# Tokens dealt four to a partition in a state-space layer gated by a GEGLU feed-forward

## The chip, the cores and the metric

The kernel runs on one core of a Trainium2 chip. The metric is the device time of one execution in microseconds (us); smaller is better. A second kind of time is used throughout: the span, from the first to the last instruction of one execution that the hardware profiler recorded.

## What is computed

x has 2048 tokens of 512 channels, in bf16. Cut to what matters, the reference is:

```python
xn = layernorm(x)                                   # per token, over 512 channels
Lam_bar = exp(dt * Lam);  B_bar = ((Lam_bar - 1) / Lam)[:, None] * B      # complex, 512 states
Bu = xn @ B_bar.T
for t in range(2048):                               # the recurrence runs over the tokens in order
    h = Lam_bar * h + Bu[t];  hs.append(h)
s = 2 * real(hs @ C.T) + xn * Dskip
g = silu((gelu(xn @ w_gate) * (xn @ w_up)) @ w_down)      # 512 -> 1376 -> 512
out = x + s * g
```

## The kernel before

The 2048 tokens are worked in four slabs of 512 (index `s`), each slab in four tiles of 128 tokens (index `m`). A tile puts its 128 tokens on the 128 partitions: before, tile `m` of slab `s` holds tokens 512s+128m to 512s+128m+127, so one partition holds one token of each tile.

- Loads. `load_x` (call at L222) brings the first slab as four transfers of one tile, `load_slab` (L217) the three others as one transfer each. Both read rows of one token, 1 KB, into `x_tok`.
- Normalized tokens go through a DMA transpose (`dma_t4`, L360) into `xnT`, channels on the partitions and tokens along the free axis, tile by tile. The first slab's feed-forward uses transposes on TensorE instead (L313, L328).
- Feed-forward, one tile after another: `gate_tile` makes the up and gate products (matmuls at L434; the first slab's are at L383 and L402), ScalarE copies them out of PSUM (L437), VectorE multiplies them (L443, L445), a DMA transpose turns the product (`at_t`, L450), and `down_pair` makes the down product (L466) and its Silu (L469).
- State part: `half(s, h)` makes, for half of the states, the products of B with all 512 tokens of the slab (matmuls at L532, one PSUM bank of 512 columns each, channels of the state on the partitions and tokens along the columns). ScalarE copies each bank into the tile `U` as bf16 (L534, eight copies in a slab, 32 in all). VectorE rotates `U` (L544, L556; L552 in the first slab) so that the recurrence becomes real, runs the scan along the tokens (L563), and rotates back into `hst`. The scan needs the tokens of `U` in their order in time.
- `y_tile` and `y_part` make y for a tile: eight matmuls (L482) whose stationary operand is the tile's 128 columns of `hst` and whose moving operand is C; a copy of the skip term stands in the bank beforehand (L478). VectorE multiplies with g (L487), adds x (L493), and a store follows (L498). The very last tile is made in two halves of 256 columns.

PSUM has eight banks: six form a ring that the products of L434, L466 and L532 take in turn, two (`ybank`) belong to y. A product can start only when the copy of the ring's former product from its bank is done. The statistics of the later slabs run on ScalarE (L744), as do their normalizations (L749).

The order of the work is written out as a list, `ORDER`, which is the same in both kernels: it fixes the sequence of instructions on every engine and in every DMA queue. TensorE is PE below, its weight loads (of stationary operands) PEld, VectorE DVE, ScalarE ACT.

Of the kernel before, what the change touches and what calls it, by code (L numbers as in the profile page):

```python
# [10 lines left out]
AF = mybir.ActivationFunctionType  # L11
# [6 lines left out]
PE, ACT, DVE, POOL, SP = "PE", "ACT", "DVE", "POOL", "SP"  # L18
# [62 lines left out]
def kernel(  # L81
# [17 lines left out]
    nc = tc.nc  # L99
    P = 128  # L100
# [5 lines left out]
    NPT = 4  # L106
    H2 = NPT // 2
    TS = 512
    NS = S // TS
    M = TS // P  # L110
# [10 lines left out]
    V, A, G, T = nc.vector, nc.scalar, nc.gpsimd, nc.tensor  # L121
    act = A.activation
# [5 lines left out]
    def sb(name, shape, dt=BF16):  # L128
        return consts.tile(shape, dt, name=name)

    x_tok = sb("x_tok", [P, NS * M, D])
# [5 lines left out]
    C2 = sb("C2", [P, 2, NPT, D])  # L137
    pv0, pv1 = sb("pv0", [4, P]), sb("pv1", [8, P])
    Drow = sb("Drow", [P, D])
    hst = [sb(f"hst{i}", [P, 2, NPT, TS]) for i in range(2)]  # L140
# [7 lines left out]
    U = [sb(f"U{i}", [P, 2, H2, TS]) for i in range(NU)]  # L148
# [11 lines left out]
    ot = [sb(f"ot{i}", [P, D]) for i in range(2)]  # L160
# [21 lines left out]
    def acts(n, emit, reads=(), writes=(), ptr=0, **kw):  # L182
        return pl.add(ACT, AC + 0.12 * ptr + n / 1200.0, emit, reads, writes, lag=0.16, **kw)
# [7 lines left out]
    def dma(eng, issue, land, emit, reads=(), writes=(), **kw):  # L191
        return pl.add(eng, issue, emit, reads, writes, lag=land, **kw)

    TURN, SLAB = (3, 2.28, 1.5), (2, 1.5, 1.0)
    x_r = A_x[0].rearrange("(m p) d -> p m d", p=P)
    out_td = out[0]
    w_of = {
        "wg": (wg, B_w_gate.rearrange("(k p) f -> p k f", p=P)),
        "wu": (wu, B_w_up.rearrange("(k p) f -> p k f", p=P)),
# [4 lines left out]
    def dma_sp(end, landed, emit, writes, **kw):  # L204

        n = dma(SP, end - sp_at[0], landed - end, emit, writes=writes, after=list(sp_last), not_before=sp_at[0], svc=(1, 0.0, 0.0), **kw)
        sp_at[0] = end
        sp_last[:] = [n]
# [5 lines left out]
               [(nm, k, c) for k in range(k0, k1) for c in range(3) if c0 <= CH[c][0] < c1])  # L214

    def load_slab(s, **kw):
        dma(SP, 0.8, 4.0, lambda: nc.sync.dma_start(out=x_tok[:, s * M : (s + 1) * M, :], in_=x_r[:, s * M : (s + 1) * M, :]),  # L217
            writes=[("x", s, m) for m in range(M)], svc=SLAB, **kw)


    def load_x(m, end, landed):
        dma_sp(end, landed, lambda: nc.sync.dma_start(out=x_tok[:, m, :], in_=x_r[:, m, :]), [("x", 0, m)])  # L222

    W2 = CH[1][1]
    load_x(0, 1.12, 2.92)
# [247 lines left out]
    def y_part(s, m, c0, c1, bank, key, seed, e):  # L473

        w = c1 - c0
        ps = bank[:, 0:w]
        if seed:
            acts(w, lambda: act(out=ps, in_=sk[s % 2][:, m, c0:c1], func=AF.Copy), [("sk", s % 2, m)], [key])  # L478

        def f():  # L480
            for j in range(2 * NPT):
                T.matmul(ps, lhsT=hst[s % 2][:, j // NPT, j % NPT, m * P : (m + 1) * P], rhs=C2[:, j // NPT, j % NPT, c0:c1],  # L482
                         start=(j == 0 and not seed), stop=(j == 2 * NPT - 1), skip_group_check=True)
        pe(2 * NPT, w, f, [("hst", s % 2, 0), ("hst", s % 2, 1)] + C2S + ([key] if seed else []), [key])
        gi, b = g2s[s, m]
        if seed:
            dve(w, lambda: V.tensor_tensor(out=yg[e][:, c0:c1], in0=ps, in1=g2[gi][:, b, c0:c1], op=ALU.mult), [key, ("g2", gi, b)], [("yg", e, c0)])  # L487
        else:
            ys = tF[:, 0, c0:c1]
            dve(w, lambda: V.tensor_tensor(out=ys, in0=ps, in1=sk[s % 2][:, m, c0:c1], op=ALU.add), [key, ("sk", s % 2, m)], [("tF",)])  # L490
            dve(w, lambda: V.tensor_tensor(out=yg[e][:, c0:c1], in0=ys, in1=g2[gi][:, b, c0:c1], op=ALU.mult), [("tF",), ("g2", gi, b)], [("yg", e, c0)])
        o = 2 + m % 2 if s == NS - 1 and m >= M - 2 else m % 2
        dve(w, lambda: V.tensor_tensor(out=ot[o][:, c0:c1], in0=yg[e][:, c0:c1], in1=x_tok[:, s * M + m, c0:c1], op=ALU.add),  # L493
            [("yg", e, c0), ("x", s, m)], [("ot", o, c0)], rate=2.0)
        mg = s * TS + m * P
        cuts = (0, HD) if (NS - 2, M - 2) <= (s, m) < (NS - 1, M - 2) else (c0,)
        for lo, hi in zip(cuts, (*cuts[1:], c1)):
            dma(SP, 0.35, 1.5, lambda lo=lo, hi=hi: nc.sync.dma_start(out=out_td[mg : mg + P, lo:hi], in_=ot[o][:, lo:hi]), [("ot", o, c0)], [("out", s, m, lo)], svc=(2, 0.4, 0.9))  # L498

    def y_tile(s, m):  # L500
        i = y_n[0] % 2
# [20 lines left out]
    def half(s, h):  # L522
        ui = u_n[0] % NU
        u_n[0] += 1
        for q in range(H2):
            pt = h * H2 + q
            for ri in range(2):
                r, ps = bank()

                def f(ri=ri, pt=pt, ps=ps):  # L530
                    for k in range(KT):
                        T.matmul(ps[:], lhsT=BT[:, ri, k, pt * P : (pt + 1) * P], rhs=xnT[:, s % 2, :, k, :], start=(k == 0), stop=(k == KT - 1))  # L532
                pe(KT, 512, f, [("BT", ri)] + [("xnT", s % 2, m) for m in range(M)], [("bank", r)])
                acts(512, lambda q=q, ri=ri, ps=ps: act(out=U[ui][:, ri, q, :], in_=ps[:], func=AF.Copy), [("bank", r)], [("U", ui, q, ri)])  # L534
        WQ = [P, 2, 2, H2 * TS]
        hs = slice(h * H2, (h + 1) * H2)
        Uf = U[ui][:].rearrange("p r q t -> p r (q t)")
        Wf = W[:].rearrange("p r q t -> p r (q t)")
        Ff = Fs[:].rearrange("p r q t -> p r (q t)")
        Qf = Q[:].rearrange("p j r q t -> p j r (q t)")  # L540
        tf = tab[:, :, hs, :].rearrange("p (j r) q t -> p j r (q t)", j=2)

        def rot(src, table, reads):
            dve(4096, lambda: V.tensor_tensor(out=Qf, in0=src.unsqueeze(1).to_broadcast(WQ), in1=table, op=ALU.mult),  # L544
                reads, ["Q"], rate=2.0)

        def turn(src, dst, reads, writes, back):
            if s == 0:
                rot(src, tf[:, :, 0, :].unsqueeze(2).to_broadcast(WQ), reads + ["tab0", "tab2"])
                for ri in range(2):  # L550
                    op = ALU.add if (ri == 0) == back else ALU.subtract
                    dve(1024, lambda ri=ri, op=op: V.tensor_tensor(out=dst[:, ri, :], in0=Qf[:, 0, ri, :], in1=Qf[:, 1, 1 - ri, :], op=op),  # L552
                        ["Q"], writes, rate=2.0)
            else:
                rot(src, tf[:, :, ::-1, :] if back else tf, reads + TABS)
                dve(2048, lambda: V.tensor_tensor(out=dst, in0=Qf[:, 0, :, :], in1=Qf[:, 1, ::-1, :], op=ALU.add), ["Q"], writes, rate=2.0)  # L556

        turn(Uf, Wf, [("U", ui, q, ri) for q in range(H2) for ri in range(2)], ["W"], True)
        for q in range(H2):
            for ri in range(2):  # L560
                pt = h * H2 + q
                first = 0.0 if s == 0 else ini[h][:, ri, q : q + 1]
                pl.add(DVE, 1.12 if s == 0 else 1.185, lambda ri=ri, q=q, pt=pt, first=first: V.tensor_tensor_scan(  # L563
                    out=Fs[:, ri, q, :], data0=rho[:, pt : pt + 1].to_broadcast([P, TS]), data1=W[:, ri, q, :], initial=first,
                    op0=ALU.mult, op1=ALU.add), ["W", "rho", ("ini", h)], [("F", ri, q)], lag=0.13)
        allf = [("F", ri, q) for ri in range(2) for q in range(H2)]
        if s < NS - 1:
            fl = Fs[:, :, :, TS - 1]
            Wc = [P, 2, H2]
            it = ini[h]  # L570

            def carry():
                V.tensor_tensor(out=ta[:], in0=fl, in1=cS[:, hs].unsqueeze(1).to_broadcast(Wc), op=ALU.mult)
                V.tensor_tensor(out=tb[:], in0=fl, in1=sS[:, hs].unsqueeze(1).to_broadcast(Wc), op=ALU.mult)
                V.tensor_tensor(out=it[:, 0, :], in0=ta[:, 0, :], in1=tb[:, 1, :], op=ALU.subtract)
                V.tensor_tensor(out=it[:, 1, :], in0=ta[:, 1, :], in1=tb[:, 0, :], op=ALU.add)
            pl.add(DVE, 0.42, carry, allf + ["trig"], [("ini", h)], lag=0.13)
        turn(Ff, hst[s % 2][:, :, hs, :].rearrange("p r q t -> p r (q t)"), allf, [("hst", s % 2, h)] + (CTS if s == 1 else []), False)
# [102 lines left out]
    c1, s1 = cbt[:, :, 1], sbt[:, :, 1]  # L681
# [32 lines left out]
    for pt in range(NPT):  # L714
# [3 lines left out]
            out=C2[:, 0, pt, :], in0=CT[:, 0, pt, :], scalar=cre[:, pt : pt + 1], in1=tF[:, 1, :], op0=ALU.mult, op1=ALU.subtract),  # L718
            ["coef", ("CT", 0), ("tF",)], [("C2", 0, pt)], base=0.13)
        dve(512, lambda pt=pt: V.scalar_tensor_tensor(  # L720
            out=C2[:, 1, pt, :], in0=CT[:, 1, pt, :], scalar=ncre[:, pt : pt + 1], in1=tF[:, 0, :], op0=ALU.mult, op1=ALU.subtract),
# [104 lines left out]
```

## Time and profile before

| what | value |
|---|---|
| median of 3 runs | 179.13 us (178.66 to 179.43) |
| the profiled execution: time, span | 178.61 us, 176.8 us |
| PE busy | 171.7 us, 97% of the span |
| weight loads busy (beside PE) | 82.7 us, 47% |
| DVE busy | 156.4 us, 88% |
| ACT busy | 125.1 us, 71% |
| granted clock of TensorE | 1.0 |
| DMA packets | 48083, 18.66 MB |

The 1.8 us between span and time lie ahead of the first and behind the last instruction. Busy shares are means over stages that differ: the first 25 us belong to the first slab's feed-forward, and the four state parts start near 24, 38, 72 and 107 us. Groups of instructions are named by line, engine and operation; a matmul's own duration includes its way through the array, while the next one starts earlier.

### The profile page before, as it was taken

The page shows a single profiled execution, that of the slowest core. Times are in us where ns is not written, and L with a number is a line of the kernel's source. Part 1 is how long each engine was busy: PE and PEld are TensorE (multiplying, and loading weights), DVE is VectorE, ACT ScalarE, POOL GpSimd, SP SyncE. Part 2 cuts the span into 40 slices and gives each one's busy share as a digit, 9 for nine tenths or more (in the row PEclk, how much of TensorE's full clock was granted, in tenths as well). Part 3 has the DMA queues.
Part 4 walks back from the last instruction along what each step waited for, and adds up shares of the span by engine and source line. Part 5 has one row for each costly group of instructions (what it writes and reads, how often), then busy time and mean ns, then how long its engine had stood idle before and what let it go on. Part 6 is the DMA issues. An engine that isn't in the chain of part 4 may idle for free.

```text
span 176.8 us, 2414 instructions
## 1 busy us (share of the span) xinstructions
PE 171.7 (97%) x834; PEld 82.7 (47%) x850; DVE 156.4 (88%) x252; ACT 125.1 (71%) x240; POOL 12.0 (7%) x25
## 2 busy tenths in 40 slices
PE   7999999999999999999999999999999999999992
PEld 2555544444455544444445454444444455444451
DVE  3829999999799993999979999899999999999764
ACT  6779999969999999799578855373158618582240
POOL 2462040000200000000040000000000000000000
PEclk9999999999999999999999999999999999999999
DMA  5999999997000809423000075094000007526022
GB/s 141 348 366 222 176 249 279 186 275 150 0 0 2 198 4 177 105 82 59 0 0 6 30 110 121 30 193 85 0 0 0 0 30 157 69 56 139 26 76 76
DMA packets 48083, 18.66 MB, mean 106 GB/s; under 512 B 40296, under 2 KB 47048, under 8 KB 48072
## 3 DMA queue, kind: packets, MB, share of 16 engines
q1 hardware_dynamic: 48048, 18.52, 47.7%
q8 instruction: 6, 0.10, 0.2%
q14 instruction: 5, 0.04, 0.1%
q10 hardware_dynamic: 24, 0.00, 0.0%
HBM read 6.46 MB, written 2.10 MB: 48 GB/s over the span
## 4 chain that ended last, share of the span: by engine, by line
PE 94%; DVE 2%; DMA 1%; issue 1%; DVEq 0%
PE ring L434 31%; PE ring L466 21%; PE ring L532 16%; PE ybank L482 15%; PE ring L402 7%; PE ring L383 3%; DMA x_tok<-in_A_x_dram 1%; PE ybank L383 1%; DVE yg L487 1%; DVE junk L493 1%; PE ybank L328 0%; DVE yg L341 0%; PE ring L313 0%; DVE xna L343 0%; PE ring L302 0%
## 5 line engine op out<-in xcount | busy, mean ns | idle before, releaser
L434 PEld LDWEIGHTS <-xnT 128*128 128x128 bf16 x288 | 28.2, 98 | 28.4
L466 PE MATMUL ring<-wd,atT 128*128 128x512 bf16 (+1 forms) x170 | 38.9, 379 | 0.3
L434 PE MATMUL ring<-wg,xnT 128*128 128x512 bf16 (+1 forms) x143 | 31.4, 357 | 0.1
L434 PE MATMUL ring<-wu,xnT 128*128 128x512 bf16 (+1 forms) x141 | 31.1, 356 | 0.2
L532 PE MATMUL ring<-xnT,BT 128*128 128x512 bf16 x128 | 30.1, 379 | 0.0
L563 DVE TENSOR_TENSOR_SCAN Fs<-rho,ini,W 128x512 bf16<-128x512 f32 x24 | 29.7, 1271 | 0.1
L437 ACT ACTIVATE ub<-ring 128x512 bf16<-128x512 f32 (+1 forms) x36 | 19.2, 555 | 14.1 <-PE ring L434 14.0
L482 PE MATMUL ybank<-C,hst 128*128 128x512 bf16 x116 | 27.3, 379 | 0.2
L466 PEld LDWEIGHTS <-atT 128*128 128x128 bf16 (+1 forms) x176 | 17.2, 98 | 20.8
L534 ACT ACTIVATE U<-ring 128x512 bf16<-128x512 f32 x32 | 18.0, 600 | 6.7 <-PE ring L532 6.7
L437 ACT ACTIVATE gt<-ring 128x512 bf16<-128x512 f32 (+1 forms) x36 | 19.5, 556 | 3.7 <-PE ring L434 3.5
L482 PEld LDWEIGHTS <-hst 128*128 128x128 bf16 x136 | 13.3, 98 | 14.0
L469 ACT ACTIVATE g<-ring 128x512 f32<-128x512 f32 x16 | 9.4, 594 | 14.3 <-PE ring L466 14.2
L532 PEld LDWEIGHTS <-BT 128*128 128x128 bf16 x128 | 12.5, 98 | 14.7
L544 DVE TENSOR_TENSOR Q<-U,tab 128x4096 bf16<-128x4096 bf16 x8 | 18.3, 2290 | 1.0 <-ACT tab L631 0.7
L544 DVE TENSOR_TENSOR Q<-Fs,tab 128x4096 bf16<-128x4096 bf16 x8 | 18.3, 2288 | 0.1
L487 DVE TENSOR_TENSOR yg<-ybank,g 128x512 bf16<-128x512 f32 x15 | 10.2, 685 | 5.4 <-PE ybank L482 5.3
L744 ACT ACTIVATE junk<-x_tok 128x512 bf16<-128x512 bf16 x16 | 10.0, 631 | 0.9 <-DMA x_tok<-in_A_x_dram 0.9
L478 ACT ACTIVATE ybank<-sk 128x512 f32<-128x512 bf16 x15 | 9.1, 605 | 1.7 <-DVE yg L487 1.6
L749 ACT ACTIVATE xna<-x_tok,nb,rs 128x512 bf16<-128x512 bf16 x12 | 9.6, 818 | 0.0
L402 PE MATMUL ring<-wg,W 128*128 128x512 bf16 (+1 forms) x47 | 9.4, 356 | 0.1
L563 DVE TENSOR_TENSOR_SCAN Fs<-rho,W 128x512 bf16<-128x512 f32 x8 | 9.3, 1210 | 0.1
(127 smaller groups left out, 170.5 us busy)
## 6 DMA issues: line engine op xcount, KB each, us to landing
x_tok<-in_A_x_dram SPq DMA_DIRECT2D x3, 512.0 KB, 7.0
wg<-in_B_w_gate_dram SPq DMA_DIRECT2D x1, 1376.0 KB, 8.1
wd<-in_B_w_down_dram SPq DMA_DIRECT2D x1, 1280.0 KB, 7.1
out_dram<-ot SPq DMA_DIRECT2D x10, 128.0 KB, 1.7
wu<-in_B_w_up_dram SPq DMA_DIRECT2D x4, 256.0 KB, 3.6
x_tok<-in_A_x_dram SPq DMA_DIRECT2D x4, 128.0 KB, 2.4
out_dram<-ot SPq DMA_DIRECT2D x8, 64.0 KB, 1.6
wu<-in_B_w_up_dram SPq DMA_DIRECT2D x1, 352.0 KB
```

Source lines behind the costliest of these rows:

```text
L402: T.matmul(ps[:, 0 : b - a], lhsT=xcT[:, k, m * P : (m + 1) * P], rhs=wt[:, k, a:b], start=(k == 0), stop=(k == KT - 1))
L434: T.matmul(ps[:, 0 : b - a], lhsT=xnT[:, s % 2, m, k, :], rhs=wt[:, k, a:b], start=(k == 0), stop=(k == KT - 1))
L437: acts(b - a, lambda: act(out=dst[:, a:b], in_=ps[:, 0 : b - a], func=AF.Copy if up else AF.Gelu_apprx_tanh), [("bank", r)], [key], table= ...
L466: T.matmul(ps[:], lhsT=atT[:fs, k, m * P : (m + 1) * P], rhs=wd[:fs, k, :], start=(k == 0), stop=(k == NFT - 1))
L482: T.matmul(ps, lhsT=hst[s % 2][:, j // NPT, j % NPT, m * P : (m + 1) * P], rhs=C2[:, j // NPT, j % NPT, c0:c1], start=(j == 0 and not seed ...
L487: dve(w, lambda: V.tensor_tensor(out=yg[e][:, c0:c1], in0=ps, in1=g2[gi][:, b, c0:c1], op=ALU.mult), [key, ("g2", gi, b)], [("yg", e, c0)])
L532: T.matmul(ps[:], lhsT=BT[:, ri, k, pt * P : (pt + 1) * P], rhs=xnT[:, s % 2, :, k, :], start=(k == 0), stop=(k == KT - 1))
L534: acts(512, lambda q=q, ri=ri, ps=ps: act(out=U[ui][:, ri, q, :], in_=ps[:], func=AF.Copy), [("bank", r)], [("U", ui, q, ri)])
L544: dve(4096, lambda: V.tensor_tensor(out=Qf, in0=src.unsqueeze(1).to_broadcast(WQ), in1=table, op=ALU.mult), reads, ["Q"], rate=2.0)
L563: pl.add(DVE, 1.12 if s == 0 else 1.185, lambda ri=ri, q=q, pt=pt, first=first: V.tensor_tensor_scan(out=Fs[:, ri, q, :], data0=rho[:, pt ...
L744: acts(512, lambda i=i, fn=fn, sc=sc, m=m: act(out=junk()[:], in_=x_tok[:, s * M + m, :], func=fn, scale=sc, accum_out=sx[:, s, i, m : m + ...
L749: acts(512, lambda m=m: act(out=xn[m], in_=x_tok[:, s * M + m, :], func=AF.Identity, scale=rs[:, s, m : m + 1], bias=nb[:, s, m : m + 1]), ...
```

## The change

Partition p of slab s now holds the four tokens 512s+4p to 512s+4p+3; tile m is every fourth token, beginning with the m-th. In the tensors in memory these four tokens are neighbours, so a slab load reads one run of 4 KB in each partition. The first slab's four loads and all stores still move rows of 1 KB (or 512 bytes), now with a step of 4 KB from partition to partition.

Everything done token by token is unaffected by which tokens form a tile. The scan, however, needs the order in time. The products of L532 come out tile by tile (column 128m+t is token 4t+m), so the copy into `U` (L534) reads the bank in order and writes with a step of four elements, in four sweeps of 128. `hst` is then in time order, and y's matmul reads its stationary operand, tile m's 128 columns, with a step of four elements. Both programs issue the same instructions in the same order on each engine; only these shapes and addresses differ.

```diff
-    x_r = A_x[0].rearrange("(m p) d -> p m d", p=P)
-    out_td = out[0]
+    x_r, out_td = (t[0].rearrange("(s p m) d -> s p m d", p=P, m=M) for t in (A_x, out))
...
     def load_slab(s, **kw):
-        ... nc.sync.dma_start(out=x_tok[:, s * M : (s + 1) * M, :], in_=x_r[:, s * M : (s + 1) * M, :]),
+        ... nc.sync.dma_start(out=x_tok[:, s * M : (s + 1) * M, :], in_=x_r[s]),
...
     def load_x(m, end, landed):
-        ... nc.sync.dma_start(out=x_tok[:, m, :], in_=x_r[:, m, :]), [("x", 0, m)])
+        ... nc.sync.dma_start(out=x_tok[:, m, :], in_=x_r[0][:, m, :]), [("x", 0, m)])
...
+        hv = hst[s % 2][:].rearrange("p r q (t m) -> p r q m t", m=M)
         def f():
             for j in range(2 * NPT):
-                T.matmul(ps, lhsT=hst[s % 2][:, j // NPT, j % NPT, m * P : (m + 1) * P], rhs=C2[:, j // NPT, j % NPT, c0:c1],
+                T.matmul(ps, lhsT=hv[:, j // NPT, j % NPT, m, :], rhs=C2[:, j // NPT, j % NPT, c0:c1],
...
-        mg = s * TS + m * P
...
-            ... nc.sync.dma_start(out=out_td[mg : mg + P, lo:hi], in_=ot[o][:, lo:hi]) ...
+            ... nc.sync.dma_start(out=out_td[s][:, m, lo:hi], in_=ot[o][:, lo:hi]) ...
...
-                acts(512, ... act(out=U[ui][:, ri, q, :], in_=ps[:], func=AF.Copy), ...)
+                acts(512, ... act(out=U[ui][:, ri, q, :].rearrange("p (t m) -> p m t", m=M),
+                                  in_=ps[:].rearrange("p (m t) -> p m t", m=M), func=AF.Copy), ...)
```

More of the change, by code (lines that the diff above doesn't have):

```diff
@@ L216, in load_slab @@
     def load_slab(s, **kw):
-        dma(SP, 0.8, 4.0, lambda: nc.sync.dma_start(out=x_tok[:, s * M : (s + 1) * M, :], in_=x_r[:, s * M : (s + 1) * M, :]),
+        dma(SP, 0.8, 4.0, lambda: nc.sync.dma_start(out=x_tok[:, s * M : (s + 1) * M, :], in_=x_r[s]),
             writes=[("x", s, m) for m in range(M)], svc=SLAB, **kw)
     def load_x(m, end, landed):
-        dma_sp(end, landed, lambda: nc.sync.dma_start(out=x_tok[:, m, :], in_=x_r[:, m, :]), [("x", 0, m)])
+        dma_sp(end, landed, lambda: nc.sync.dma_start(out=x_tok[:, m, :], in_=x_r[0][:, m, :]), [("x", 0, m)])
     W2 = CH[1][1]
@@ L494, in y_part @@
             [("yg", e, c0), ("x", s, m)], [("ot", o, c0)], rate=2.0)
-        mg = s * TS + m * P
         cuts = (0, HD) if (NS - 2, M - 2) <= (s, m) < (NS - 1, M - 2) else (c0,)
         for lo, hi in zip(cuts, (*cuts[1:], c1)):
-            dma(SP, 0.35, 1.5, lambda lo=lo, hi=hi: nc.sync.dma_start(out=out_td[mg : mg + P, lo:hi], in_=ot[o][:, lo:hi]), [("ot", o, c0)], [("out", s, m, lo)], svc=(2, 0.4, 0.9))
+            dma(SP, 0.35, 1.5, lambda lo=lo, hi=hi: nc.sync.dma_start(out=out_td[s][:, m, lo:hi], in_=ot[o][:, lo:hi]), [("ot", o, c0)], [("out", s, m, lo)], svc=(2, 0.4, 0.9))
     def y_tile(s, m):
@@ L533, in half @@
                 pe(KT, 512, f, [("BT", ri)] + [("xnT", s % 2, m) for m in range(M)], [("bank", r)])
-                acts(512, lambda q=q, ri=ri, ps=ps: act(out=U[ui][:, ri, q, :], in_=ps[:], func=AF.Copy), [("bank", r)], [("U", ui, q, ri)])
+                acts(512, lambda q=q, ri=ri, ps=ps: act(out=U[ui][:, ri, q, :].rearrange("p (t m) -> p m t", m=M), in_=ps[:].rearrange("p (m t) -> p m t", m=M), func=AF.Copy), [("bank", r)], [("U", ui, q, ri)])
         WQ = [P, 2, 2, H2 * TS]
```

## The prediction

> **What bounds the kernel now.** I began with the page's busy times and its chain that ended last.
>
> ```profile
> PE 171.7 (97%) x834; PEld 82.7 (47%) x850; DVE 156.4 (88%) x252; ACT 125.1 (71%) x240; POOL 12.0 (7%) x25
> PE 94%; DVE 2%; DMA 1%; issue 1%; DVEq 0%
> ```
>
> PE carries the end. Whether it waits anywhere is seen in the chain in order of time: start, length, work.
>
> ```profile
> 0.72 2.21 DMA x_tok<-in_A_x_dram
> 71.58 6.04 PE ring L532 x28
> 155.41 1.73 PE ybank L482 x8
> 171.94 0.70 DVE yg L487
> ```
>
> 28 matmuls in 6.04 us are 216 ns each, and so are 8 in 1.73 us. From 4.1 us to 171.9 us the chain shows PE work and pieces of "issue" of 0.05 us, nothing else: PE runs at 216 ns per 512 columns without a hole. So the change can gain only ahead of 4.1 us (the first load and what follows it) and behind 171.9 us (the last tile's vector work and stores). Everything else can only lose, by making PE slower or by making it wait.
>
> Next, the groups by shape that the change touches (count, busy us, mean ns, idle before), and the copies of another width for a slope.
>
> ```profile
> L534 ACT ACTIVATE U<-ring 128x512 bf16<-128x512 f32 x32 | 18.0, 600 | 6.7 <-PE ring L532 6.7
> L482 PEld LDWEIGHTS <-hst 128*128 128x128 bf16 x136 | 13.3, 98 | 14.0
> L482 PE MATMUL ring<-C,hst 128*128 128x256 bf16 x16 | 1.9, 272 | 0.0
> L437 ACT ACTIVATE gt<-ring 128x512 bf16<-128x512 f32 x24 | 14.2, 601 | 1.8 <-PE ring L434 1.8
> L437 ACT ACTIVATE gt<-ring 128x352 bf16<-128x352 f32 x12 | 5.6, 465 | 1.9 <-PE ring L434 1.7
> ```
>
> Then busy time in stretches that I cut around the eight `U` copies of each slab (slab 0's start at 25.8 to 33.0, slab 1's at 40.8 to 51.7, slab 2's at 72.5 to 92.3, slab 3's at 111.5 to 131.8).
>
> ```profile
> core 0: us, PE busy (x) PEld busy (x) DVE busy (x) ACT busy (x) POOL busy (x), PEclk, DMA share, GB/s
> 24.30:37.70 13.40, 13.35 (x63) 6.06 (x62) 13.16 (x18) 11.45 (x21) 1.05 (x1) 1.00 1.07 243
> 37.70:52.80 15.10, 15.05 (x73) 7.12 (x73) 13.88 (x21) 15.07 (x33) 1.01 (x1) 1.00 0.40 82
> 72.20:93.00 20.80, 20.69 (x100) 9.75 (x100) 19.55 (x28) 16.71 (x37) 1.84 (x1) 1.00 0.17 39
> 93.00:132.00 39.00, 38.79 (x186) 18.40 (x189) 37.87 (x50) 21.39 (x40) 0.00 (x0) 1.00 0.33 65
> ```
>
> ACT's mean of 71% hides that from 37.7 to 52.8 it is busy 15.07 of 15.10 us. Last, the transfers (size, median us to landing).
>
> ```profile
> x_tok<-in_A_x_dram SPq DMA_DIRECT2D x3, 512.0 KB, 7.0
> out_dram<-ot SPq DMA_DIRECT2D x10, 128.0 KB, 1.7
> x_tok<-in_A_x_dram SPq DMA_DIRECT2D x4, 128.0 KB, 2.4
> out_dram<-ot SPq DMA_DIRECT2D x8, 64.0 KB, 1.6
> L744 ACT ACTIVATE junk<-x_tok 128x512 bf16<-128x512 bf16 x16 | 10.0, 631 | 0.9 <-DMA x_tok<-in_A_x_dram 0.9
> ```
>
> **Part by part.** The instruction order on every engine and queue stays as it is, so no step is moved past another; only prices can change.
>
> *Slab loads (3).* 512 runs of 1 KB become 128 of 4 KB. Bounds on each: no change, or down from 7.0 us to about 3.5 (2.4 for a tile alone, plus three more tiles, 0.39 MB at the 366 GB/s of the page's busiest slice, 1.1 us). What waits for them is ACT's first L744, 0.9 us in one place, just ahead of 37.7. Earlier landing starts ACT's full stretch up to 0.9 us sooner; PE does not wait there now, so this gains 0. What is next in the queue (BT, the transposes) lands earlier, also ahead of a PE that never waits. Value 0; it only builds cover.
>
> *First-slab loads (4) and stores (21).* Same number of rows, now 4 KB apart. The first load is on the path (0.72 to 2.93 us). No row here has this step; the nearest is the half-tile store, whose 512-byte runs stand 1 KB apart and which lands in 1.6 us against 1.7 for a store without gaps. So I take 0, with 0.3 us either way for head and tail together.
>
> *Weight loads of y (136).* On 120 of them the next one starts 216 ns later, so a load of 98 ns has 118 ns of shadow; on the last tile's 16 the matmuls are 109 ns apart ((1.91 us - 0.27) / 15 in the timeline) and the shadow is 11 ns. No strided weight load is in the trace. Bounds: nothing, or one element at a time at the far row of the 4-element vector operations that read with a step (157 ns at L573 against 148 at L700, contiguous: 2.2 ns an element), 128 x 2.2 = 0.28 us more, 0.38 us a load: 120 x (0.38 - 0.216) + 16 x (0.38 - 0.109) = 24 us. I stay at the row that is the same instruction, 98 ns, with 22 ns on it for the new addresses: 120 loads remain in shadow, and the last 16 stand out by 11 ns each, 0.2 us at the end of the chain. If that cover were gone, each ns above 216 costs 0.12 us.
>
> *`U` copies (32).* 512 elements are read in order and written 8 bytes apart. The slope from 352 to 512 columns is (600 - 465) / 160 = 0.84 ns an element: one element per slot on the reading side, whatever the output. Bounds: 0, or the far row again, 512 x 2.2 = 1.1 us a copy. I take 0, since the copy works at one element a slot already and 2-byte results leave the write side half empty; four sweeps instead of one add little (I allow 5 ns, 8 x 5 = 0.04 us in the stretch that counts). [...]
>
> *DVE.* It reads `U`, writes `hst` as before: 0. A later `U` would reach L544, which idles 1.0 us in all ahead of `U`.
>
> Sum against the profiled execution: 178.61 + 0.2 (last tile) = 178.8. That execution lay 0.52 below the median of the runs, so 179.3 in their terms.
>
> **Rivals.**
>
> *A, the copies pay for the step (slower).* Each element written to a place of its own takes two slots: 512 x 0.84 = 0.43 us more per copy, 3.45 us per slab. From 37.7 to 52.8 ACT has 0.03 us free, so slab 1 pays all: 3.4. Slab 0 has 13.40 - 11.45 = 1.95 free and pays 1.5. Slab 2 has 4.1, slab 3 17.6: nothing. Sum 4.9: 184.2. The ring does not hide it: the first of slab 1's products, written from 38.53, is copied at 40.76, 1.4 us after its four matmuls, so the banks stand full and PE waits next at L532 and L434. It decides from 0.9 / 8 = 0.11 us per copy on. For: no free time, and no row that shows such a write. Against: the same engine reaches the same 600 ns whether its output is bf16 or (L469, 594) twice as wide. [...]
>
> *B, the weight loads outgrow their shadow (slower).* At twice 98 ns only the last tile pays: 16 x (196 - 109) = 1.4 us, 180.5. At 2.5 times: 120 x 29 + 16 x 136 = 5.7 us, 184.8; at three times 12.4 us, 191.5. [...] Against: 98 ns is the same for 128 rows and for 96 (L466), so much of it looks fixed.
>
> *C, the head (slower).* The first tile's rows 4 KB apart land 1 us later, all of it on the path: 180.3. Against: the gapped stores.
>
> *D, faster.* Head and tail gain together: x lands 0.5 us earlier and the last stores too; 178.2 at best, since PE's 168 us stand between.
>
> *E, nothing happens at all:* the transfers are cut into the same packets and the steps cost nothing; 179.1.
>
> **How the numbers follow.** My forecast has 0.40, E 0.04, A 0.33, B 0.12, C 0.05, D 0.06. A measurement of this kernel can tell about 0.5%, 0.9 us, from no change: same 0.44 (forecast, E), slower 0.50 (A, B, C), faster 0.06. The single likeliest case is the forecast, 179.3, and its own range is 178.6 to 180.0. As cases of both signs hold the chance, the whole range goes from D's 178.2 up past A's 184.2 and B's 184.8, to 185.0; it leaves out B's upper part and an A of more than two slots.
>
> **What would show it.** Right: the L534 group stays at 600 ns, the L482 weight loads under 120 ns, the chain has no piece but PE between 4.1 and 171.9 us, L744's wait for x shrinks, packets fall by about 3 x 384. Wrong by A: L534 above 710 ns, waits of PE for ACT at L532 and L434 from 38 to 65 us. Wrong by B: weight loads above 216 ns and y's eight matmuls above 1.73 us. Wrong by C: PE's first transpose later than 4.1 us.

## The result, and the profile after

The changed kernel takes 189.84 us (median of 6 runs, 189.62 to 192.22) against 179.00 for the one before on the same chip: ratio 1.063, 95% interval 1.058 to 1.069, 10.8 us slower. The forecast was no change (179.3, range up to 185.0). The direction of rival A came true, at more than its price. The profiled execution of the changed kernel took 189.74 us, its span is 188.0 us, 11.2 more than before. In some executions TensorE's products at the start stay 427 ns apart in place of 216 for longer and 0.7 to 2.5 us are added (the profiled ones of e2, e3 and e8 are of that kind), and medians and ratios include them.

The page after, busy times and the chain that ended last; many line numbers moved by one (the `U` copies from L534 to L533).

```profile
PE 174.4 (93%) x834; PEld 84.5 (45%) x850; DVE 156.8 (83%) x252; ACT 144.9 (77%) x240; POOL 14.5 (8%) x25
PE 60%; ACT 33%; issue 2%; DVE 2%; DMA 1%; DVEq 0%
```

PE had 94% of the chain, now 60%, and ACT has a third of it. ACT is busy 144.9 - 125.1 = 19.8 us longer with the same 240 instructions. The groups by shape say which:

```profile
L533 ACT ACTIVATE U<-ring 128x512 bf16<-128x512 f32 x32 | 40.2, 1354 | 3.7 <-PE ring L531 3.7
L482 PEld LDWEIGHTS <-hst 128*128 128x128 bf16 x136 | 15.4, 113 | 12.8 <-issue 0.8
L743 ACT ACTIVATE junk<-x_tok 128x512 bf16<-128x512 bf16 x16 | 10.1, 644 | 0.0
```

The `U` copies went from a mean of 600 ns to 1354 and from 18.0 to 40.2 us in all. The weight loads went from 98 to 113. The wait of the statistics for x (0.9 us before, at L744) is gone; e1 and e2 show why. Busy time in the stretches shown before:

```profile
core 0: us, PE busy (x) PEld busy (x) DVE busy (x) ACT busy (x) POOL busy (x), PEclk, DMA share, GB/s
24.30:37.70 13.40, 12.94 (x61) 5.87 (x60) 11.91 (x16) 13.40 (x17) 3.51 (x2) 1.00 0.88 204
37.70:52.80 15.10, 11.95 (x54) 5.16 (x53) 10.12 (x16) 15.07 (x28) 1.01 (x1) 1.00 0.58 114
72.20:93.00 20.80, 20.21 (x95) 9.46 (x94) 17.64 (x23) 20.29 (x31) 0.00 (x0) 1.00 0.56 91
```

From 24 to 53 us ACT is busy all but 0.03 us, and PE, which had worked 15.05 of 15.10 us in the second stretch, works 11.95. The chain in order of time shows the hand-over: start, length, work.

```profile
21.93 2.42 PE ring L401 x11
33.07 2.35 ACT U L533 x2
48.80 2.33 ACT U L533 x2
55.56 2.34 ACT U L533 x2
61.28 9.94 PE ring L433 x49
84.77 3.50 ACT U L533 x3
124.72 2.46 ACT U L533 x2
141.86 1.75 ACT U L533 x2
```

There are pieces with `U` copies in all four state parts, also in the one that starts after 107 us. The transfers after (size, median us to landing):

```profile
x_tok<-in_A_x_dram SPq DMA_DIRECT2D x3, 512.0 KB, 6.6
out_dram<-ot SPq DMA_DIRECT2D x10, 128.0 KB, 1.9
x_tok<-in_A_x_dram SPq DMA_DIRECT2D x4, 128.0 KB, 2.6
out_dram<-ot SPq DMA_DIRECT2D x8, 64.0 KB, 1.7
```

Slab loads land 0.4 us earlier here, but that is inside their spread: 6.5 to 7.2 us in the experiments below that leave them as they were, 6.6 to 6.8 in those with runs of 4 KB. Stores, whose rows are now 4 KB apart, land 0.1 to 0.2 us later. The very first load takes 2.44 us in the chain in place of 2.21; the median of the first slab's four loads moves by 0.2 us too, but it is 2.1 to 2.6 in experiments with the old rows. Packets fell from 48083 to 46931, by 1152 = 3 x 384, as the runs of 4 KB ask.

### The profile page after: what moved, and what is told of

It reads as the page before. It is cut to its first block, busy times and chain, and to the rows that moved or that the text cites. A ratio compares the mean times of both kernels' runs of the same rounds, so it can differ in the third digit from the quotient of the medians.

```text
span 188.0 us, 2414 instructions
## 1 busy us (share of the span) xinstructions
PE 174.4 (93%) x834; PEld 84.5 (45%) x850; DVE 156.8 (83%) x252; ACT 144.9 (77%) x240; POOL 14.5 (8%) x25
## 2 busy tenths in 40 slices
DMA packets 46931, 18.66 MB, mean 99 GB/s; under 512 B 40296, under 2 KB 45512, under 8 KB 46920
## 4 chain that ended last, share of the span: by engine, by line
PE 60%; ACT 33%; issue 2%; DVE 2%; DMA 1%; DVEq 0%
PE ring L433 23%; ACT U L533 17%; PE ybank L482 13%; PE ring L465 10%; PE ring L401 6%; ACT junk L743 4%; PE ring L531 3%; PE ring L382 3%; ACT g L468 3%; ACT L468 2%; ACT L436 1%; DMA x_tok<-in_A_x_dram 1%; ACT gt L436 1%; ACT xna L748 1%; ACT ub L436 1%
## 5 line engine op out<-in xcount | busy, mean ns | idle before, releaser
L433 PEld LDWEIGHTS <-xnT 128*128 128x128 bf16 x288 | 28.1, 98 | 36.9 <-issue 9.9
L533 ACT ACTIVATE U<-ring 128x512 bf16<-128x512 f32 x32 | 40.2, 1354 | 3.7 <-PE ring L531 3.7
L465 PE MATMUL ring<-wd,atT 128*128 128x512 bf16 (+1 forms) x170 | 39.0, 379 | 0.9 <-ACT U L533 0.6
L433 PE MATMUL ring<-wg,xnT 128*128 128x512 bf16 (+1 forms) x143 | 31.7, 356 | 4.2 <-ACT U L533 3.0
L433 PE MATMUL ring<-wu,xnT 128*128 128x512 bf16 (+1 forms) x141 | 31.5, 356 | 2.6 <-ACT U L533 1.8
L482 PE MATMUL ybank<-C,hst 128*128 128x512 bf16 x116 | 27.5, 379 | 0.7 <-ACT ybank L477 0.5
L465 PEld LDWEIGHTS <-atT 128*128 128x128 bf16 (+1 forms) x176 | 17.2, 98 | 21.7 <-issue 1.1
L436 ACT ACTIVATE gt<-ring 128x512 bf16<-128x512 f32 (+1 forms) x36 | 20.0, 571 | 2.8 <-PE ring L433 2.6
L482 PEld LDWEIGHTS <-hst 128*128 128x128 bf16 x136 | 15.4, 113 | 12.8 <-issue 0.8
L743 ACT ACTIVATE junk<-x_tok 128x512 bf16<-128x512 bf16 x16 | 10.1, 644 | 0.0
```

The lines of the kernel that those rows point to most:

```text
L433: T.matmul(ps[:, 0 : b - a], lhsT=xnT[:, s % 2, m, k, :], rhs=wt[:, k, a:b], start=(k == 0), stop=(k == KT - 1))
L436: acts(b - a, lambda: act(out=dst[:, a:b], in_=ps[:, 0 : b - a], func=AF.Copy if up else AF.Gelu_apprx_tanh), [("bank", r)], [key], table= ...
L465: T.matmul(ps[:], lhsT=atT[:fs, k, m * P : (m + 1) * P], rhs=wd[:fs, k, :], start=(k == 0), stop=(k == NFT - 1))
L482: T.matmul(ps, lhsT=hv[:, j // NPT, j % NPT, m, :], rhs=C2[:, j // NPT, j % NPT, c0:c1], start=(j == 0 and not seed), stop=(j == 2 * NPT - ...
L743: acts(512, lambda i=i, fn=fn, sc=sc, m=m: act(out=junk()[:], in_=x_tok[:, s * M + m, :], func=fn, scale=sc, accum_out=sx[:, s, i, m : m + ...
```

## The experiments

My theory after the result: the write of single 2-byte results, 8 bytes apart, is the whole loss; its rival, that loads, stores and y's stepped operand share in it.

**e1: the stepped copies alone.** The kernel before, with this edit:

```diff
-  act(out=U[ui][:, ri, q, :], in_=ps[:], func=AF.Copy)
+  act(out=U[ui][:, ri, q, :].rearrange("p (t m) -> p m t", m=M), in_=ps[:].rearrange("p (m t) -> p m t", m=M), func=AF.Copy)
```

> The kernel before with one edit: the U copies write with a step of four elements (in four sweeps of 128), loads, stores and y's operand as before; the tokens of U are therefore out of order in time. Theory 1 (the stepped write of ScalarE is the whole cost): a U copy takes 1.30 to 1.45 us as in the changed kernel, total 189 to 190.5. Theory 2 (a large part comes from the gapped loads and stores or from y's stepped weight loads): total under 187, the rest missing.

Measured: 189.91 us (before 178.88), ratio 1.061, interval 1.059 to 1.063.

```profile
L534 ACT ACTIVATE U<-ring 128x512 bf16<-128x512 f32 x32 | 40.3, 1358 | 3.7 <-PE ring L532 3.7
L744 ACT ACTIVATE junk<-x_tok 128x512 bf16<-128x512 bf16 x16 | 10.1, 640 | 0.0
L482 PEld LDWEIGHTS <-hst 128*128 128x128 bf16 x136 | 13.3, 98 | 14.7 <-issue 0.8
```

The copies alone give the whole loss, and ACT the same 3.7 us of idle time before them, with plain weight loads. The statistics (L744) do not wait for x here either, although the slab loads are the old ones: ACT comes to the first of them at 40.7 us in place of 37.7, when x has landed.

**e2: everything but the stepped copies.** The changed kernel with the edit of e1 undone.

> The changed kernel with the U copies written contiguously as before; 4 KB slab loads, gapped loads and stores and y's stepped weight loads stay; the scan therefore runs over tokens out of order. Theory 1: U copies back at 0.60 us, total 178.5 to 179.8 (the head 0.2 later by the first load, the last tile's 16 weight loads at 113 ns a few ns over 109 each). Theory 2: above 181.

Measured: 179.21 us, ratio 1.002, interval 1.000 to 1.004.

```profile
PE 94%; DVE 2%; DMA 1%; issue 1%; DVEq 0%
L533 ACT ACTIVATE U<-ring 128x512 bf16<-128x512 f32 x32 | 18.2, 602 | 6.8 <-PE ring L531 6.7
L482 PEld LDWEIGHTS <-hst 128*128 128x128 bf16 x136 | 15.4, 113 | 12.1
L743 ACT ACTIVATE junk<-x_tok 128x512 bf16<-128x512 bf16 x16 | 10.0, 633 | 0.7 <-DMA x_tok<-in_A_x_dram 0.7
```

Loads, stores and stepped weight loads together cost at most 0.4%; the weight loads take the same 113 ns as in the changed kernel. The rival falls. With 4 KB runs but short copies, the statistics (L743) still wait 0.7 us for x, against 0.9 before.

**e3: the step on the reading side.** The changed kernel, its copy with the loops turned round:

```diff
-  act(out=U[ui][:, ri, q, :].rearrange("p (t m) -> p m t", m=M), in_=ps[:].rearrange("p (m t) -> p m t", m=M), func=AF.Copy)
+  act(out=U[ui][:, ri, q, :].rearrange("p (t m) -> p t m", m=M), in_=ps[:].rearrange("p (m t) -> p t m", m=M), func=AF.Copy)
```

> The changed kernel with the loops of the U copy turned round: it writes U contiguously in time order and reads the PSUM bank with a step of 128 elements (one token of each tile in turn); the result is the full computation. Theory 1a (only a stepped 2-byte write to SBUF pays): copy 0.60 us, total 178.7 to 179.8. Theory 1b (ScalarE pays for any step, read or write): copy 1.0 us or more, total 184 or more.

Measured: 178.95 us, ratio 1.0035, interval 0.9994 to 1.0076.

```profile
L533 ACT ACTIVATE U<-ring 128x512 bf16<-128x512 f32 x32 | 18.2, 602 | 6.8 <-PE ring L531 6.7
```

The same elements go from the same places to the same places; only the order differs. Reading PSUM with 512 bytes between neighbours costs ScalarE nothing (602 against 600 ns); writing with 8 bytes between neighbours costs 0.75 us a copy. So theory 1a holds.

**e4: the order put right by TensorE.** The changed kernel with plain copies and

```diff
-  T.matmul(ps[:], lhsT=BT[...], rhs=xnT[:, s % 2, :, k, :], ...)
+  T.matmul(ps[:], lhsT=BT[...], rhs=xnT[:, s % 2, :, k, :].rearrange("p m t -> p t m"), ...)
```

> The changed kernel with the order put right one step earlier: the moving operand of U's matmuls is read in time order (four tokens 1 KB apart, then the next four), so that bank and U are in time order and the copies are plain; the full computation. If TensorE reads such an operand at full rate: matmuls 216 ns apart, total 178.7 to 179.8. If each element costs a second slot: 128 matmuls of 430 ns, 27 us more, 206.

Measured: 275.52 us, ratio 1.536, interval 1.532 to 1.540. Neither number was right: the chain in order of time of the kernel before has these matmuls 216 ns apart; here the starts of neighbours are 865 ns apart, four times that, or 1.7 ns an element. It is the same where the granted clock is 1.00 (216.7 to 220.1 us, four matmuls in 3.46 us) and where it is 0.50 (126 to 141 us, inside a piece of 28 in 24.20 us).

```profile
L531 PE MATMUL ring<-xnT,BT 128*128 128x512 bf16 x128 | 113.1, 1041 | 0.0
```

128 x 0.649 = 83 us of the 96.6 (99.2 between the profiled spans) are these matmuls. Most of the rest is other matmuls at a lower clock: the granted clock is 0.839 in the mean over the span, and in the chain of the profiled execution the products of L433, L465 and L482 take about 15 us longer than those of L434, L466 and L482 before. Four of L465 behind the first run of 32, at a granted clock of 0.50, take 1.71 us in place of 0.86.

**e5: four steps side by side.** The kernel before with `o` for the tile's slice; the copies of a half are, in turn,

```diff
-  act(out=U[ui][:, ri, q, :], in_=ps[:], func=AF.Copy)
+  lambda o=o, ps=ps: act(out=o.rearrange("p (t m) -> p m t", m=2), in_=ps[:].rearrange("p (m t) -> p m t", m=2), func=AF.Copy),   # L536
+  ...                                                                # L537: m=4, L538: m=8, L539: m=16
```

> The kernel before with the four U copies of each half written with four different steps, 2, 4, 8 and 16 elements (4, 8, 16, 32 bytes), each on a line of its own; tokens of U are out of order. Read by the mean of each line's copies. Theory W (a new 8-byte word for each result costs, results that share a word do not): step 2 about 0.60 to 0.65 us, steps 4, 8 and 16 all 1.3 us. Theory N (any 2-byte result without its neighbour costs, because results go out two at a time): step 2 also 1.3 us, all four alike. Theory D (the cost grows with the distance): 0.6, 1.3, and clearly more at 8 and 16. Total 186 to 191 in any case.

Measured: 203.39 us, one run (my range for the total was too low). The copies of each line, min/median/max ns:

```profile
L536 ACT ACTIVATE U<-ring x8: 739/782/1091, 26.8 to 145.7; 128x512 bf16<-128x512 f32 x8
L537 ACT ACTIVATE U<-ring x8: 1301/1314/1367, 30.2 to 142.7; 128x512 bf16<-128x512 f32 x8
L538 ACT ACTIVATE U<-ring x8: 2434/2458/2834, 27.4 to 153.3; 128x512 bf16<-128x512 f32 x8
L539 ACT ACTIVATE U<-ring x8: 2335/2420/2709, 31.9 to 155.2; 128x512 bf16<-128x512 f32 x8
```

The totals of e5 and e6 are from one run each; the copies' own times carry the argument. None of W, N and D fits: already 4 bytes apart costs something, the cost still doubles from 8 to 16 bytes, and there it stops. My estimate from these medians: the four fit a price per 16-byte piece visited. With 600 - 512 x 0.84 = 170 ns as the fixed part of a copy (from the 465 and 600 ns at 352 and 512 columns before), what is left is 612 ns for 128 pieces (4.8 ns each), 1144 for 256 (4.5), 2288 for 512 (4.5) and 2250 for 512 (4.4).

**e6: runs in place of single elements.** As e5, but the pattern is `"p (t m b) -> p m t b"` with runs of b elements: L536 m=2, b=2; L537 m=2, b=4; L538 m=4, b=2; L539 m=4, b=4.

> The kernel before with the four U copies of each half written in runs: two elements every 8 bytes, four every 16 bytes (both in two sweeps), two every 16 bytes, four every 32 bytes (both in four sweeps); tokens of U are out of order. Theory N: 0.60 us for all four, total 178.5 to 179.5. Theory W: runs of four fill a word, 0.60 us; runs of two pay for half as many words as single elements, about 0.96 us. If only the number of sweeps or rows mattered, runs of two and four would both stay near 1.3 us.

Measured: 179.22 us, one run.

```profile
L536 ACT ACTIVATE U<-ring x8: 587/597/622, 26.4 to 124.3; 128x512 bf16<-128x512 f32 x8
L537 ACT ACTIVATE U<-ring x8: 572/598/619, 28.6 to 121.0; 128x512 bf16<-128x512 f32 x8
L538 ACT ACTIVATE U<-ring x8: 627/650/686, 26.9 to 132.0; 128x512 bf16<-128x512 f32 x8
L539 ACT ACTIVATE U<-ring x8: 585/606/619, 29.8 to 132.5; 128x512 bf16<-128x512 f32 x8
```

Two neighbours together are enough: pairs 8 bytes apart cost nothing, pairs 16 bytes apart 50 ns a copy, although they visit 256 pieces of 16 bytes, as the single elements of e5's L537 do for 1314 ns. So neither the step, nor the sweeps, nor the visit to a new piece is dear by itself, but, as far as these patterns go, a 2-byte result written without its neighbour, by the estimate above at about 4.5 ns for each 16-byte piece in which that happens. All pairs here begin at an even element; others were not run. N named the condition, and its price (all steps alike) was wrong. Why the hardware does so, the runs do not show.

**e7 and e8: one slab alone.** The kernel before with the edit of e1 only where s == 1, or only where s == 3.

> The kernel before with stepped U copies (1.32 to 1.45 us) in slab 1 alone, out of order there; loads, stores and y as before. Slab 1's eight copies stand in the stretch where ACT has 0.03 us free: by both theories (sums over stretches, or local backlog behind six banks) about 8 x 0.75 = 6.0 us more, 184.3 to 185.3. If the stepped copies were hidden behind full banks anyway: under 181.

> The same in slab 3 alone, where the stretch from 93 to 132 us leaves ACT 17.6 us free. Theory S (sums over stretches, as in the prediction): nothing, 178.4 to 179.4. Theory B (local backlog: the copies come in bursts close to other copies and six banks of 0.86 us cannot cover them): 1 to 2.5 us, 180 to 181.5.

Measured: 183.61 us for slab 1 (182.87 and 184.35; ratio 1.025, interval 1.015 to 1.035) and 181.85 for slab 3 (180.88 and 182.82; ratio 1.015, interval 1.002 to 1.028). In the profiled executions the spans are 181.1 and 179.1 against 176.8; e8's first run of products starts at 6.78 us in its chain, 0.67 later than before, so slab 3 costs about 2.3 - 0.7 = 1.6, slab 1 4.3. With two runs each, 1.5 and 1.9 us apart, these sizes are rough.

```profile
115.93 2.47 ACT U L534 x2
120.79 1.21 ACT U L534
133.06 1.74 ACT U L534 x2
```

These are pieces of e8's chain: with 17.6 us of free time in its stretch, slab 3's copies still stand on the path, beside a load of an activation table (L469, 1.28 us at 118.90 us). Theory B holds: free time in a long stretch does not cover a burst. Slab 1 costs 4.3 and not 8 x 0.72 = 5.8: the stretch behind it, 52.8 to 72.2, which the prediction left out, had 19.40 - 18.49 = 0.9 us free before, into which the backlog can run. That was argued, not separated, and about half a microsecond stays unexplained.

**e9: the first slab as before.** A version with the full computation: e3's copies, but slab 0 in its old order, loads, stores, copies and y.

```diff
+    dealt = [t[0].rearrange("(s p m) d -> s p m d", p=P, m=M) for t in (A_x, out)]
+    plain = [t[0].rearrange("(s m p) d -> s p m d", p=P, m=M) for t in (A_x, out)]
+    x_r, out_td = ([plain[i][0] if s == 0 else dealt[i][s] for s in range(NS)] for i in range(2))
```

> A version of its own, the full computation: slab 0 keeps its tokens 128 to a tile (its loads, stores, copies and y as before), slabs 1 to 3 have tokens dealt four to a partition, 4 KB loads, y's stepped weight loads, and U copies that write contiguously and read the bank with a step. Theory H (what the kernel with stepped bank reads loses against the one before, in about a third of its runs 2.4 us, comes from the first tile landing later by its rows 4 KB apart, so that TensorE's clock drops back before the first product): no run above 179.6, median 178.5 to 179.0, ratio 0.998 to 1.001. Theory T (it comes from the stores or from the later slabs): runs near 181 stay. Neither expects it to beat the kernel before by 0.5%, since TensorE has no hole to fill.

Measured: 179.10 us (before 179.09), ratio 1.001, interval 0.9986 to 1.0035; one run of 12 at 181.22, which H had ruled out. As expected there is nothing to win: with ACT relieved, PE again carries 94% of the chain.

**e10: the first loads alone.** The kernel before with its first four loads in rows 4 KB apart (`x_d = A_x[0][0:TS].rearrange("(p m) d -> p m d", m=M)`).

> The kernel before with its first four loads alone reading rows 4 KB apart; everything else, the stores too, is as before, so that tokens of slab 0 meet the wrong places on the way out. The first load should land near 3.15 us instead of 2.74 to 2.93. Theory H1 (the later landing is all): every run 0.2 to 0.4 us longer, 179.2 to 179.5, none at 181. Theory H2 (the later landing lets TensorE's clock stay low for longer in part of the runs): about one run in four near 181, the others 179.0 to 179.5. If neither load nor clock matters: median 178.9 to 179.1, ratio 1.000.

Measured: 179.18 us (before 179.01), ratio 1.002, interval 0.9994 to 1.0051; two runs of 12 near 181. The first load is again 0.2 us longer than the 2.21 before:

```profile
0.72 2.40 DMA x_tok<-in_A_x_dram
```

Runs near 181 (or their like) came in 7 of 38 with the gapped first load (after, e2, e3, e10), in 1 of 12 of e9 and in none of the 62 runs of before beside all experiments. That speaks for H2 against H1. But the traces record from when on the granted clock is 1.0: from 4.3 us before, 4.4 after, 6.1 to 6.4 in e2, e4 and e10 and 9.8 in e3, yet also only from 5.1 to 6.4 in e1, e5, e6, e7 and e8, whose first loads are the old ones. So a later first load is not needed for a late rise, and what part it has stays open.

## Why the prediction was wrong, point by point

- *What bounds it* was right: PE without a hole, nothing to gain, only ways to lose. ACT's full stretch behind a mean of 71% was the place: slab 1 alone costs 4.3 us of the 11 (e7).
- *The `U` copies, value 0*: this is the step that failed. I argued that one element a slot on the reading side sets the pace whatever the output, and that the write side stands half empty; that was my estimate from copies without a step (600 ns with bf16 results, 594 at L469 with results twice as wide), and no row showed it for stepped results. The copy took 1323 ns (median) in place of 597, and the runs put the price on the writing side: stepped writes alone cost the whole 11 us (e1), the same permutation with a stepped read costs nothing (e3). The far row's bound, 1.1 us more, held it; I took the other end, without a row for it. Four bytes apart the copy still takes 782 ns, and by the estimate from e5 the price goes with the 16-byte pieces, but the visit to a new piece alone is not dear: e6's pairs 16 bytes apart visit as many pieces as the single elements of e5's L537, for 50 ns a copy.
- *Rival A* named the copies as the cause, the condition (0.11 us a copy) and the place; its term was mis-sized. Two slots would be 0.43 us more per copy; measured 0.72. By its own sum 0.72 gives 5.7 for slab 1, 3.8 for slab 0, 1.7 for slab 2, 0 for slab 3, 11.2 in all against 11.0 measured in e1. That agreement is partly luck: e7 and e8 give 4.3 and 1.6 where the sum has 5.7 and 0, and slabs 0 and 2 were not run alone. What its two slots a result missed is that adjacent pairs run free or nearly so (597 to 650 ns, e6), while lone elements 4 to 32 bytes apart take 782 to 2458 ns (e5).
- *Weight loads*: right. 113 ns where I put 120, all in shadow; e2 has the step and runs as before, and the last tile's 16 matmuls take 1.91 us there as before, so the 0.2 us put on them did not come. Rival B falls.
- *Slab loads*: value 0 was right. The gain in landing was small (7.0 to 6.6 us), and it is not what took away ACT's 0.9 us wait: with these loads alone 0.7 of it stays (e2), with the stepped copies alone it is gone (e1).
- *First load, stores (0, up to 0.3 us either way)*: 0.1 to 0.2 us later each. Rival C's 1 us as a steady loss falls; e2 and e10 put the whole at 0.2%, 0.3 to 0.4 us at the edge of the bound, with intervals that hold no change at all.
- *The range* ended at 185.0 because A was held to two slots, though the part on the copies had a far bound of 1.1 us a copy.

## What to carry to other kernels

When a copy changes the order of elements, put the step on the side that reads PSUM and let ScalarE's 2-byte writes to SBUF run in neighbours, at least in pairs (597 to 650 ns a copy in e6): the same permutation cost 0.75 us a copy one way and nothing the other. Price such a copy on the engine that makes it, in the stretch in which it stands, not by the mean load; bursts can cost even where the stretch has time to spare (about 1.6 us in slab 3, e8). And where no row shows an operation, the bound of the far row belongs into the range, not only into the text.

## What the runs showed of the hardware

- ScalarE writing single bf16 results to SBUF: 782, 1314, 2458 and 2420 ns for 512 columns at 4, 8, 16 and 32 bytes apart, 600 without a gap, 597 to 650 in runs of two or four.
- ScalarE reading fp32 from PSUM with 512 bytes between neighbours: 602 ns, as without.
- TensorE's stationary operand with a step of 8 bytes: 113 ns against 98, hidden. Its moving operand with 1 KB between neighbours: 865 ns apart against 216, at a granted clock of 1.00 and of 0.50 alike (e4).
- TensorE at the start: after the dummy matmuls half the rate (427 ns apart against 216) can last. In e3's profiled execution (span 179.3 us), whose granted clock is 1.0 only from 9.8 us on, the first six products of a run of 22 take 2.76 us, where the kernel before makes all 22 in 4.75:

```profile
7.13 2.76 PE L382 MATMUL ring<-wu,W 128*128 128x512 bf16 x6
```

What decides how long it lasts was not found.
